# The order of the SBUF tiles in a dynamic convolution with two products behind it

## The chip, the cores and the metric

The kernel runs on one core of a Trainium2 chip. The metric is the device time of one execution in microseconds (us). It is given as the median of three runs.

## What is computed

The input `x` has 16384 tokens (4 sequences of 4096) of 192 channels. For each token and each of 8 heads a softmax over 7 weights is formed, and the token's 24 channels of the head become the weighted sum of the last 7 tokens (zeros ahead of a sequence). The result goes through two matrix products with a pointwise function between them, of 192 to 2048 to 192 channels:

```python
w = np.exp(w); w = w / (np.sum(w, axis=-1, keepdims=True) + 1e-09)
out = np.einsum('bshk,bskhg->bshg', w, x_unf)        # 7 taps
h = x @ w_in
g = np.where(h >= 1, h, np.where(h <= -1, 0.0, (h + 1) ** 2 / 4.0))
return (g @ w_out).astype(np.float32)
```

`w_in` and `w_out` come as 8-byte floats, all else as float32.

## The kernel before

**Tiling.** The tokens are cut into 32 blocks of 512, the 2048 hidden channels into 16 chunks of 128. A step of the main loop (index `w`) handles a pair of chunks of one block, so that there are 256 pairs, 8 for a block. Precision beyond one pass comes from splits into two parts: `hc` and `hl` are the high and low part of a block's transposed rows, `whi` and `wlo` those of `w_in`, `wo` holds both parts of `w_out` (192 + 192 columns for a chunk), `gh` and `gl` those of the hidden values.

**The first product** (`gemm1_pair`, L378) runs 9 passes for a pair: three thirds of the channels (64 rows each), and for each `whi` with `hc`, `wlo` with `hc`, `whi` with `hl`. A pass is two matmuls of 512 columns, one on either half of the array's rows. The weights are the operand that is loaded (128 columns, 512 bytes of a partition), `hc` or `hl` is the moving one (2048 bytes).

**The second product** (`gemm2_part`, L432) comes two pairs later. It runs 16 passes for a pair, again two matmuls each: `gh` is loaded and 384 columns of `wo` move (1536 bytes), then `gl` is loaded and 192 columns move. Two such passes are called a round here; there are 8 rounds for a pair.

**The other engines.** Between the two products ScalarE takes relu and square (L389, L392) and writes `gh` (L403), VectorE combines (L397) and writes `gl` (L404). GpSimd forms the convolution of a later block (L179, L189), VectorE transposes it in parts, SyncE issues all DMAs. In the first pairs the weights are decoded besides: 8 chunk buffers' worth of 8-byte floats are loaded into four buffers `r` (pool `raw`), and ScalarE and VectorE turn them into `whi`, `wlo` and `wo` by way of `head` and a PSUM bank `psw` (L327, L331, L340, L352, L356).

**What sets the order.** The order of each engine is written out by hand (`tc.manual_schedule()`), the tiles' buffers rotate within their pools.

**Where tiles lie.** The pools are laid out one behind another in the order in which they are opened, and within a pool the tiles in the order in which they are first asked for; each tile takes its bytes of a partition, rounded up to 32. The buffer `warm`, one float32, takes 32 bytes so, and what follows it starts at an odd multiple of 32.

Of the kernel before, what the change touches and what calls it, by code (L numbers as in the profile page):

```python
# [10 lines left out]
F32 = mybir.dt.float32  # L11
F32R = mybir.dt.float32r
U32 = mybir.dt.uint32
U16 = mybir.dt.uint16
BF16 = mybir.dt.bfloat16
F16 = mybir.dt.float16
AF = mybir.ActivationFunctionType
# [5 lines left out]
def kernel(  # L23
# [21 lines left out]
    nc = tc.nc  # L45
    P = 128
    B, S, D = x.shape
# [6 lines left out]
    Q = P // 2  # L54
# [18 lines left out]
    group_of = {b: (g, i) for g, bs in enumerate(groups) for i, b in enumerate(bs)}  # L73

    const = ctx.enter_context(tc.tile_pool(name="const", bufs=1))
    raw = ctx.enter_context(tc.tile_pool(name="raw", bufs=4))
    xp = ctx.enter_context(tc.tile_pool(name="xp", bufs=2))
    wp = ctx.enter_context(tc.tile_pool(name="wp", bufs=2))
    sp = ctx.enter_context(tc.tile_pool(name="sp", bufs=2))
# [2 lines left out]
    up = ctx.enter_context(tc.tile_pool(name="up", bufs=3))  # L82
    gp = ctx.enter_context(tc.tile_pool(name="gp", bufs=6))
    op = ctx.enter_context(tc.tile_pool(name="op", bufs=2))
    dram = ctx.enter_context(tc.tile_pool(name="dram", bufs=2, space=bass.MemoryType.DRAM))
    ps_h = ctx.enter_context(tc.tile_pool(name="ps_h", bufs=4, space=bass.MemoryType.PSUM))
    ps_o = ctx.enter_context(tc.tile_pool(name="ps_o", bufs=1, space=bass.MemoryType.PSUM))
# [2 lines left out]
    wr = wg.rearrange("b s h k -> (b s) (h k)")  # L90

    ident = const.tile([P, P], F32, tag="ident", name="ident")
    warm = const.tile([P, 1], F32, tag="warm", name="warm")
    ident16 = const.tile([P, P], BF16, tag="ident16", name="ident16")
    heads = [const.tile([P, (D // Q) * P + 2 * D, 2], U16, tag=f"head{m}", name="head") for m in range(2)]
    whi = const.tile([P, NF // 2, NC, P], F32R, tag="whi", name="whi")
    wlo = const.tile([P, NF // 2, NC, P], F32R, tag="wlo", name="wlo")
    wo = const.tile([P, NF, 2, D], F32R, tag="wo", name="wo")

    def run(ops):  # L100
        for o in ops:
            o()
# [28 lines left out]
    def load_w(g):  # L131
        bs = groups[g]
        t0, nb = bs[0] * N, len(bs)
        t = wp.tile([P, 2, n, H, K], F32, tag="w", name="w")
        nc.sync.dma_start(
            out=t[:, 0:nb].rearrange("p b j h k -> p b (j h k)"),
            in_=wr[t0:t0 + nb * N, :].rearrange("(b p j) e -> p b (j e)", p=P, j=n))
        w_t[g] = t
# [392 lines left out]
    with tc.manual_schedule():  # L531
        for t in heads:
            nc.vector.memset(t, 0)
        nc.gpsimd.memset(warm, 0.0)
        nc.scalar.activation(out=warm, in_=warm, func=AF.Exp)
        load_w(0)
        load_w(1)
        clear_x(0)
# [211 lines left out]
```

## Time and profile before

| | |
|---|---|
| runs | 1160.29, 1160.81, 1160.94 us |
| median | 1160.81 us |
| span of the profiled execution, first to last instruction | 1158.6 us |
| busy share of the span | PE 99%, weight loads 90%, ScalarE 83%, VectorE 72%, GpSimd 68% |
| granted TensorE clock | 1.00 in all but the first and last stretch |

The profile comes from one execution. Its own time from end to end is not given apart; its span is 2.2 us under the median of the runs. A matmul's busy time includes the stretch in which it drains beside the next one, so the distance from one start to the next, and not the duration, is a pass's share of the time.

### The profile page before, as it was taken

What the parts mean: (1) busy time and instruction counts of PE and PEld (TensorE: products, weight loads), DVE (VectorE), ACT (ScalarE), POOL (GpSimd) and SP (SyncE); (2) the same over time, 40 slices, a digit from 0 to 9 for tenths busy, and PEclk for the clock granted to TensorE, in tenths of its full rate; (3) what the DMA queues carried; (4) which work ended last, traced back from release to release, by engine and by line L of the source; (5) the groups of instructions that cost most, each with busy time, mean ns of one, the idle gap of its engine ahead of it and who ended that gap; (6) DMA issues with size and microseconds to landing.
All of it is one profiled execution on the core that took longest, in us unless ns stands there. A gap on an engine that the chain in (4) does not pass through costs nothing.

```text
span 1158.6 us, 32197 instructions
## 1 busy us (share of the span) xinstructions
PE 1145.0 (99%) x12885; PEld 1038.1 (90%) x12885; DVE 834.1 (72%) x1271; ACT 964.7 (83%) x1745; POOL 792.5 (68%) x511
## 2 busy tenths in 40 slices
PE   7999999999999999999999999999999999999998
PEld 5799999999999999999999999999999999999997
DVE  8887767677676776767777676776767767677664
ACT  6878888888888888888888888888888888888886
POOL 4788976667857678486686866678576785866310
PEclk9999999999999999999999999999999999999999
DMA  9422222212222212222121222222222122221100
GB/s 229 112 82 79 77 84 90 89 64 73 75 77 90 84 61 82 71 87 90 56 89 59 85 89 90 64 73 74 76 90 95 51 85 70 80 90 57 47 24 15
DMA packets 84052, 91.43 MB, mean 79 GB/s; under 512 B 5056, under 2 KB 75712, under 8 KB 83904
## 3 DMA queue, kind: packets, MB, share of 16 engines
q1 hardware_dynamic: 83904, 89.39, 24.0%
q8 instruction: 101, 1.65, 0.6%
q14 instruction: 47, 0.39, 0.1%
HBM read 64.99 MB, written 24.38 MB: 77 GB/s over the span
## 4 chain that ended last, share of the span: by engine, by line
PE 95%; ACT 2%; DMA 2%; DVE 1%; issue 0%; POOL 0%; DVEq 0%; POOLq 0%; ACTq 0%; SPq 0%
PE o L432 48%; PE psh L378 45%; DMA r<-in_moe_w_in_dram 1%; PE psx L267 1%; DMA r<-in_moe_w_out_dram 1%; PE psx L208 0%; ACT u L392 0%; DVE psh L397 0%; ACT u L389 0%; ACT gh L403 0%; DVE psw L340 0%; DVE gl L404 0%; POOL piece L189 0%; POOL acc L189 0%; ACT hc L258 0%
## 5 line engine op out<-in xcount | busy, mean ns | idle before, releaser
L432 PE MATMUL o<-wo,gh 64*128 64x384 f32 x4096 | 612.2, 355 | 1.5 <-SPq L441 1.4
L397 DVE SCALAR_TENSOR_TENSOR psh<-u,psh 128x512 f32<-128x512 f32 x512 | 354.7, 696 | 299.6 <-ACT u L392 299.4
L432 PE MATMUL o<-wo,gl 64*128 64x192 f32 x4096 | 542.7, 251 | 0.0
L432 PEld LDWEIGHTS o<-wo,gh 64*128 64x128 f32 x4096 | 421.1, 184 | 13.1 <-SPq L441 2.3
L432 PEld LDWEIGHTS o<-wo,gl 64*128 64x128 f32 x4096 | 421.3, 187 | 9.0
L389 ACT ACTIVATE u<-psh 128x512 f32<-128x512 f32 x512 | 301.5, 589 | 93.2 <-PE psh L378 91.2
L404 DVE TENSOR_TENSOR gl<-psh,gh 128x512 fp32r<-128x512 f32 x512 | 345.7, 686 | 15.3 <-ACT gh L403 1.1
L403 ACT ACTIVATE gh<-psh 128x512 fp32r<-128x512 f32 x512 | 299.2, 592 | 65.5 <-DVE psh L397 65.5
L378 PE MATMUL psh<-hc,whi 64*128 64x512 f32 x1536 | 349.8, 404 | 3.7 <-DVE wlo L356 1.9
L189 POOL TENSOR_TENSOR acc<-acc,pr 128x768 f32<-128x768 f32 x185 | 343.8, 1858 | 5.7 <-DVE head L331 2.0
L378 PE MATMUL psh<-hl,whi 64*128 64x512 f32 x1536 | 337.7, 391 | 0.0
L378 PE MATMUL psh<-hc,wlo 64*128 64x512 f32 x1536 | 337.3, 390 | 0.0
L392 ACT ACTIVATE u<-u 128x512 f32<-128x512 f32 x512 | 323.7, 632 | 16.0
L179 POOL TENSOR_TENSOR pr<-x,w 128x768 f32<-128x768 f32 x186 | 286.8, 1549 | 7.1 <-DVE psw L340 7.1
L259 POOL TENSOR_TENSOR hl<-XT,hc 128x512 fp32r<-128x512 f32 x90 | 115.4, 1297 | 221.2 <-ACT hc L258 221.2
L378 PEld LDWEIGHTS psh<-hl,whi 64*128 64x128 f32 x1536 | 173.6, 185 | 34.7 <-DVE hl L259 0.3
L378 PEld LDWEIGHTS psh<-hc,whi 64*128 64x128 f32 x1536 | 173.0, 185 | 29.4 <-DVE wlo L356 4.3
L378 PEld LDWEIGHTS psh<-hc,wlo 64*128 64x128 f32 x1536 | 174.1, 187 | 21.4
L179 POOL TENSOR_TENSOR acc<-x,w 128x768 f32<-128x768 f32 x31 | 47.9, 1547 | 72.5 <-DVE w L155 70.6
L258 ACT ACTIVATE hc<-XT 128x512 fp32r<-128x512 f32 x90 | 55.5, 618 | 0.0
L284 DVE STREAM_TRANSPOSE T<-acc 128x768 f32<-128x768 f32 x30 | 50.9, 1698 | 0.3 <-POOL acc L189 0.3
L457 DVE SCALAR_TENSOR_TENSOR osb<-o,osb 128x384 f32<-128x384 f32 x64 | 32.7, 556 | 2.7 <-ACT osb L456 2.7
(44 smaller groups left out, 188.8 us busy)
## 6 DMA issues: line engine op xcount, KB each, us to landing
x<-in_x_dram SPq DMA_DIRECT2D x28, 960.0 KB
XT<-D SPq DMA_DIRECT2D x180, 128.0 KB
out_dram<-osb SPq DMA_DIRECT2D x31, 384.0 KB
D<-T SPq DMA_DIRECT2D x30, 384.0 KB
x<-in_x_dram SPq DMA_DIRECT2D x4, 945.0 KB
w<-in_weight_gen_dram SPq DMA_DIRECT2D x15, 224.0 KB
r<-in_moe_w_in_dram SPq DMA_DIRECT2D x16, 192.0 KB
r<-in_moe_w_out_dram SPq DMA_DIRECT2D x8, 384.0 KB
```

Of the source, the lines that this page charges most:

```text
L179: held(eng.tensor_tensor(out=t, in0=xtile[:, k:k + n, :].rearrange("p j (h g) -> p j h g", h=H), in1=wt[:, gi, :, :, k:k + 1].to_broadcast ...
L189: held(eng.tensor_tensor(out=o, in0=s, in1=t, op=ALU.add))
L258: ops.append(lambda c=c: nc.scalar.activation(out=hc[:, c], in_=src[c], func=AF.Copy))
L259: ops.append(lambda c=c: lows.append(engines[c].tensor_tensor(out=hl[:, c], in0=src[c], in1=hc[:, c].bitcast(F32), op=ALU.subtract)))
L284: lambda: nc.vector.transpose(out=T.rearrange("p b c j -> p b j c"), in_=acc.rearrange("p j (r b) -> p b j r", b=R)),
L378: nc.tensor.matmul(out=pair[h][:, 0:N], lhsT=l[rows, f // 2, (c + h) % NC if b < 2 else c], rhs=r[rows, c], start=(s == 0), stop=(s == len ...
L389: nc.scalar.activation(out=u_t[i], in_=h_t[i][:, 0:N], func=AF.Relu, scale=0.5 * UNIT, bias=0.5)
L392: nc.scalar.activation(out=u_t[i], in_=u_t[i], func=AF.Square, scale=UNIT ** -0.5)
L397: nc.vector.scalar_tensor_tensor(out=pv, in0=uv, scalar=1.0 / UNIT, in1=pv, op0=ALU.min, op1=ALU.max)
L403: nc.scalar.activation(out=gh[:, 0:N], in_=gv, func=AF.Copy)
L404: nc.vector.tensor_tensor(out=gl[:, 0:N], in0=gv, in1=gh[:, 0:N].bitcast(F32), op=ALU.subtract)
L432: mm = nc.tensor.matmul(out=o_t[b][turn][:, k, 0:cols], lhsT=g_t[i][l][rows, t * P:(t + 1) * P], rhs=wo[rows, f].rearrange("p s d -> p (s ...
```

## The change

Three things are reordered, and one tile is widened. The pool of chunk buffers is opened last of the SBUF pools, so that it lies behind all others. In the pool of constants `ident16` comes ahead of `warm`, and the two `head` tiles behind the weights. `warm` grows from 1 to 32 floats, of which one is still used. No instruction is added or taken away, the order and the waits of each engine are the same, and so are all other sizes and numbers of buffers.

```diff
     const = ctx.enter_context(tc.tile_pool(name="const", bufs=1))
-    raw = ctx.enter_context(tc.tile_pool(name="raw", bufs=4))
     xp = ctx.enter_context(tc.tile_pool(name="xp", bufs=2))
...
     op = ctx.enter_context(tc.tile_pool(name="op", bufs=2))
+    raw = ctx.enter_context(tc.tile_pool(name="raw", bufs=4))
...
     ident = const.tile([P, P], F32, tag="ident", name="ident")
-    warm = const.tile([P, 1], F32, tag="warm", name="warm")
     ident16 = const.tile([P, P], BF16, tag="ident16", name="ident16")
-    heads = [const.tile([P, (D // Q) * P + 2 * D, 2], U16, tag=f"head{m}", name="head") for m in range(2)]
+    warm = const.tile([P, 32], F32, tag="warm", name="warm")
     whi = const.tile([P, NF // 2, NC, P], F32R, tag="whi", name="whi")
     wlo = const.tile([P, NF // 2, NC, P], F32R, tag="wlo", name="wlo")
     wo = const.tile([P, NF, 2, D], F32R, tag="wo", name="wo")
+    heads = [const.tile([P, (D // Q) * P + 2 * D + 0, 2], U16, tag=f"head{m}", name="head") for m in range(2)]
...
-        nc.gpsimd.memset(warm, 0.0)
-        nc.scalar.activation(out=warm, in_=warm, func=AF.Exp)
+        nc.gpsimd.memset(warm[:, 0:1], 0.0)
+        nc.scalar.activation(out=warm[:, 0:1], in_=warm[:, 0:1], func=AF.Exp)
```

Where the tiles start in the two built programs, in bytes of a partition (the first buffer, and the remainder that all buffers of the tile share):

| tile | before | remainder | after | remainder |
|---|---|---|---|---|
| `whi`, `wlo`, `wo` | 23456, 35744, 48032 | 416 mod 512 | 17408, 29696, 41984 | 0 mod 512 |
| `head` | 17312 | 416 mod 512 | 66560 | 0 mod 512 |
| `x`, `acc`, `pr`, `T` | 97312, 123936, 130080, 117792 | 32 mod 512 | 72704, 99328, 105472, 93184 | 0 mod 512 |
| `hc`, `hl` | 139296, 151584 | 32 mod 2048 | 114688, 126976 | 0 mod 2048 |
| `XT`, `u`, `piece` | 163872, 170016, 200736 | 32 mod 2048 | 139264, 145408, 176128 | 0 mod 2048 |
| `gh`, `gl` | 176160, 188448 | 32 mod 2048 | 151552, 163840 | 0 mod 2048 |
| the four `r` | 72608, 78784, 84960, 91136 | 32, 0, 32, 0 mod 64 | 202752, 208928, 215104, 221280 | 0, 32, 0, 32 mod 64 |

## Rows read from the trace of the kernel before

**Rows 1.** The page: span, and busy us (share of the span) xinstructions.

```profile
span 1158.6 us, 32197 instructions
PE 1145.0 (99%) x12885; PEld 1038.1 (90%) x12885; DVE 834.1 (72%) x1271; ACT 964.7 (83%) x1745; POOL 792.5 (68%) x511
```

**Rows 2.** The page: the chain that ended last, by engine and by line.

```profile
PE 95%; ACT 2%; DMA 2%; DVE 1%; issue 0%; POOL 0%; DVEq 0%; POOLq 0%; ACTq 0%; SPq 0%
PE o L432 48%; PE psh L378 45%; DMA r<-in_moe_w_in_dram 1%; PE psx L267 1%; DMA r<-in_moe_w_out_dram 1%; PE psx L208 0%; ACT u L392 0%; DVE psh L397 0%; ACT u L389 0%; ACT gh L403 0%; DVE psw L340 0%; DVE gl L404 0%; POOL piece L189 0%; POOL acc L189 0%; ACT hc L258 0%
```

**Rows 3.** Stretches: busy us of each engine, clock, DMA share and GB/s.

```profile
core 0: us, PE busy (x) PEld busy (x) DVE busy (x) ACT busy (x) POOL busy (x), PEclk, DMA share, GB/s
20.00:62.00 42.00, 37.60 (x361) 30.54 (x359) 37.36 (x68) 35.88 (x70) 29.95 (x19) 1.00 0.57 122
62.00:200.00 138.00, 137.65 (x1559) 126.31 (x1558) 100.50 (x150) 116.22 (x211) 112.45 (x71) 1.00 0.26 87
200.00:600.00 400.00, 400.00 (x4562) 366.47 (x4560) 287.77 (x434) 337.81 (x610) 293.12 (x188) 1.00 0.23 77
600.00:1000.00 400.00, 400.00 (x4560) 363.73 (x4558) 287.28 (x434) 337.49 (x608) 282.21 (x181) 1.00 0.23 78
```

**Rows 4.** Timeline of PE over one pair: start us, us, engine, line, operation.

```profile
600.22 0.42 PE L378 MATMUL psh<-hc,whi 64*128 64x512 f32 x2
600.48 0.39 PE L378 MATMUL psh<-hc,wlo 64*128 64x512 f32 x2
600.71 0.40 PE L378 MATMUL psh<-hl,whi 64*128 64x512 f32 x2
...
602.11 0.40 PE L378 MATMUL psh<-hl,whi 64*128 64x512 f32 x2
602.34 0.34 PE L432 MATMUL o<-wo,gh 64*128 64x384 f32 x2
602.51 0.25 PE L432 MATMUL o<-wo,gl 64*128 64x192 f32 x2
602.60 0.36 PE L432 MATMUL o<-wo,gh 64*128 64x384 f32 x2
602.80 0.25 PE L432 MATMUL o<-wo,gl 64*128 64x192 f32 x2
602.89 0.36 PE L432 MATMUL o<-wo,gh 64*128 64x384 f32 x2
...
604.61 0.42 PE L378 MATMUL psh<-hc,whi 64*128 64x512 f32 x2
```

**Rows 5.** The same for the weight loads, from the end of the first product.

```profile
602.11 0.19 PEld L432 LDWEIGHTS o<-wo,gh 64*128 64x128 f32 x2
602.34 0.19 PEld L432 LDWEIGHTS o<-wo,gl 64*128 64x128 f32 x2
602.52 0.19 PEld L432 LDWEIGHTS o<-wo,gh 64*128 64x128 f32 x2
602.62 0.19 PEld L432 LDWEIGHTS o<-wo,gl 64*128 64x128 f32 x2
602.80 0.19 PEld L432 LDWEIGHTS o<-wo,gh 64*128 64x128 f32 x2
602.91 0.19 PEld L432 LDWEIGHTS o<-wo,gl 64*128 64x128 f32 x2
```

**Rows 6.** By tile (`wo`, `r`): duration ns min/median/max, first and last start us.

```profile
L432 PEld LDWEIGHTS o<-wo,gh x4096: 182/184/189, 24.8 to 1152.9; 64*128 64x128 f32 x196
L432 PE MATMUL o<-wo,gh x4096: 332/358/444, 25.0 to 1153.1; 64*128 64x384 f32 x196
L432 PEld LDWEIGHTS o<-wo,gl x4096: 183/188/189, 25.0 to 1153.5; 64*128 64x128 f32 x196
...
L340 DVE SCALAR_TENSOR_TENSOR psw<-r,head x16: 555/558/580, 12.5 to 49.4; 128x384 uint32<-128x384 uint32 x16
L327 ACT ACTIVATE head<-r x7: 627/642/646, 11.8 to 48.2; 128x384 f16<-128x384 bf16 x7
```

## The prediction

> **What bounds the kernel now.** I read the busy shares first: TensorE (PE) is busy for 1145.0 of 1158.6 us, ScalarE for 83% and VectorE for 72% [rows 1]. The chain of waits agrees: 95% of the span is PE, 48% of it on the second product (L432) and 45% on the first (L378), so nearly nothing else ends a wait [rows 2]. [...] Only from 20 to 62 us is it busy for just 37.60 of 42.00 us, with DVE (37.36) and ACT (35.88) as full as PE [rows 3]. So what counts is the pace of PE in the steady part, and a little the work of DVE and ACT in the first 62 us.
>
> The steady pace is that of one pair of hidden chunks, 50 matmuls. The timeline has one pair start at 600.22 and the next at 604.61 [rows 4], 4.39 us. As a cross-check, 400 us hold 4562 matmuls, or 91.2 pairs, which is 4.38 us each [rows 3]; 256 pairs of 4.387 make 1123 of the 1158.6 us. Inside a pair: from 600.48 to 602.34 stand eight passes of the first product, two matmuls of 512 columns at once in each, so (602.34 - 600.48) / 8 = 0.2325 us a pass. The second product takes 604.61 - 602.34 = 2.27 us for eight rounds of a 384-column pass (gh) and a 192-column pass (gl), 0.284 a round. The first gh pass after the first product takes 602.51 - 602.34 = 0.17; the later ones 602.80 - 602.60 = 0.20, then gl 0.09 [rows 4]. The rows of the weight loads say why: the load for the next gh starts with the gl pass (602.52 and 602.80), the load behind it follows 0.10 to 0.11 us later (602.62, 602.91), so one load occupies the loader for about 0.11 us, longer than gl's 0.09. In the second product gl is thus hidden under a load, and every round costs a load plus a gh pass; in the first product a load (0.11) has half of a pass (0.23) to spare [rows 5].
>
> **The change part by part.** No instruction is added, removed or moved, and no wait: each engine's order is the same in both programs, every queue's too (SP's and POOL's DMAs and semaphores among them), and every tile has the same size and the same number of buffers. All that differs is where a tile starts. Before, every operand of the steady loop starts at 32 bytes past a multiple of 64, because the 4-byte tile `warm` took 32; the weights `whi`, `wlo`, `wo` lie at 416 past a multiple of 512, `hc`, `hl`, `gh`, `gl` at 32 past a multiple of 2048. After, these remainders are 0. The cost is therefore a price per read or write of each engine, times its count.
>
> PE, moving rows (`hc`, `hl` in the first product, `wo` in the second). The smallest unit for which the change can matter is 64 bytes, 16 float32 columns. [...] The trace gives no row of a moving float32 operand at another remainder mod 64, so this isn't excluded. What speaks against it: `wo` lies at four remainders mod 2048 as the chunk goes on (928, 416, 1952, 1440), a 384-column read crosses a multiple of 2048 from some and not from others, and the 4096 gh matmuls still have one duration (median 358 ns, of all their pairs) [rows 6]. The pairs' equal pace at 4.38 whatever ACT, DVE, POOL and DMA do at the time says that PE's reads meet no one else's. I take 0, as the nearest rows show no dependence on an address, with 17 x 6.7 x 256 = 29 us of gain as the bound on one side.
>
> PE, weights. The loads (0.10 to 0.11 us for 128 columns) [rows 5] are on the path in the second product alone. A gain there would need a load shorter than that; a loss would need a longer one (below). I take 0.
>
> [...]
>
> ACT, DVE and POOL. The chunk buffers are the one tile of the program that lies at both remainders before (32, 0, 32, 0 mod 64, read from 2 to 4 bytes further on). The 16 VectorE reads of them that write `psw` take 555 to 580 ns, median 558, the 7 ScalarE ones 627 to 646 [rows 6]: no two groups, a spread of under 4.5%. So the durations of these engines stay, in the decode stage from 20 to 62 us too, where they are on the path. If all their work on the path there changed by that spread, it would be under 2 us of 42; I take 0 with 1 us either way. In the steady part ACT has 400 - 337.8 = 62 us of slack in 400 [rows 3], which covers any such change. The DMAs write to other addresses; from 62 us on their engines are 23 to 26% busy [rows 3] and everything they load is used pairs later, so a change there is hidden.
>
> The sum: 0, against the profiled span of 1158.6 us, which lies 2.2 us under the median of 1160.81. Forecast **1160.8 us**.
>
> **The rivals.** [...] (b) **Slower: weights and moving rows now begin on the same remainder.** Before, a weight row starts 384 bytes (mod 512) away from a moving row; after, 0. If the two reads of PE then met and a load were stretched by one of its eight 64-byte units, that is 0.11 / 8 = 13.7 ns. In the first product the half-pass of slack swallows it; in the second every load behind gl is on the path from the first ns on: 8 x 13.7 x 256 = 28 us, 1188.9 us. For it: the load is the tightest link of the round [rows 5]. Against: loads and passes advance at different speeds (0.11 us for 128 columns, 0.23 for 512), so equal starts don't keep them equal, and passes of three lengths all meet loads now without a visible stretch: loads last 182 to 189 ns in all of the rows [rows 6]. [...] That the change doesn't do what it says is no rival: the built program has the tiles where the words put them.
>
> **How the numbers follow.** No change 0.57; (a) 0.28, since a fixed cost of the right size is there and unexplained; (b) 0.15. A measurement of this kernel tells about 0.2% (2.3 us) from no change. The no-change case with its 1 us at the start lies inside that. Range: from (a)'s one-unit time, 1131, to 1163, the upper edge of no change; it leaves out (b) and the two-unit form of (a), under 0.2. The forecast's own range is 1159 to 1163. Faster 0.28, within 0.2% 0.57, slower 0.15.
>
> **What would show it.** Right: the pair's step stays 4.39 us, a first-product pass 0.2325, a round 0.284, loads 0.10 to 0.11 apart. [...] (b): first-product passes unchanged, loads over 0.11 apart behind gl, rounds near 0.30. The prediction is wrong also if DVE's or POOL's durations move enough to show in the 5.2 us per pair of the first 62 us.

## The result and the profile after

The changed kernel takes 1146.94 us (median of 4 runs, 1145.49 to 1147.49), the kernel before 1160.70 us beside it. The ratio is 0.9874, with a 95% interval of 0.9861 to 0.9887: 13.8 us or 1.26% faster. The time lies inside the predicted range, but the likeliest case, no change, did not come about.

The page of the changed kernel, span and busy us, beside [rows 1]:

```profile
span 1145.6 us, 32197 instructions
PE 1130.8 (99%) x12885; PEld 1053.4 (92%) x12885; DVE 833.7 (73%) x1271; ACT 964.4 (84%) x1745; POOL 792.3 (69%) x511
```

The same instructions run, and DVE, ACT and POOL need the same time as before to within 0.4 us. PE's busy time falls by 14.2 us, the span by 13.0. By stretches (columns as in [rows 3]):

```profile
core 0: us, PE busy (x) PEld busy (x) DVE busy (x) ACT busy (x) POOL busy (x), PEclk, DMA share, GB/s
20.00:62.00 42.00, 37.77 (x343) 31.56 (x345) 36.40 (x68) 35.81 (x70) 28.81 (x19) 0.92 0.55 123
200.00:600.00 400.00, 400.00 (x4626) 388.16 (x4624) 291.62 (x441) 342.63 (x618) 296.98 (x189) 1.00 0.24 78
600.00:1000.00 400.00, 400.00 (x4618) 366.10 (x4616) 290.57 (x439) 342.87 (x618) 289.55 (x185) 1.00 0.24 79
```

PE is as full as before, and gets through 4618 to 4626 matmuls in 400 us where it was 4560 to 4562. Its timeline over one pair, to be laid beside [rows 4] (start us, us, operation):

```profile
599.55 0.41 PE L378 MATMUL psh<-hc,whi 64*128 64x512 f32 x2
599.81 0.40 PE L378 MATMUL psh<-hc,wlo 64*128 64x512 f32 x2
600.04 0.39 PE L378 MATMUL psh<-hl,whi 64*128 64x512 f32 x2
600.27 0.39 PE L378 MATMUL psh<-hc,whi 64*128 64x512 f32 x2
600.50 0.39 PE L378 MATMUL psh<-hc,wlo 64*128 64x512 f32 x2
...
601.40 0.39 PE L378 MATMUL psh<-hl,whi 64*128 64x512 f32 x2
601.63 0.33 PE L432 MATMUL o<-wo,gh 64*128 64x384 f32 x2
601.80 0.25 PE L432 MATMUL o<-wo,gl 64*128 64x192 f32 x2
601.89 0.36 PE L432 MATMUL o<-wo,gh 64*128 64x384 f32 x2
602.09 0.25 PE L432 MATMUL o<-wo,gl 64*128 64x192 f32 x2
602.17 0.36 PE L432 MATMUL o<-wo,gh 64*128 64x384 f32 x2
...
603.88 0.41 PE L378 MATMUL psh<-hc,whi 64*128 64x512 f32 x2
```

The first product takes 601.63 - 599.55 = 2.08 us (before 602.34 - 600.22 = 2.12), the second 603.88 - 601.63 = 2.25 (before 2.27), the pair 4.33 (before 4.39). From the fourth pass on (600.27) a pass of the first product takes (601.63 - 600.27) / 6 = 0.227 us, where the mean was 0.2325. The weight loads, beside [rows 5]:

```profile
601.80 0.19 PEld L432 LDWEIGHTS o<-wo,gh 64*128 64x128 f32 x2
601.91 0.19 PEld L432 LDWEIGHTS o<-wo,gl 64*128 64x128 f32 x2
602.09 0.19 PEld L432 LDWEIGHTS o<-wo,gh 64*128 64x128 f32 x2
602.20 0.19 PEld L432 LDWEIGHTS o<-wo,gl 64*128 64x128 f32 x2
```

They follow one another by 0.11 us after a gl pass has begun, as before. So the loads are no shorter; the passes are.

With the single starts of the trace, which are kept to 1 ns, the step from pair to pair can be had to 1 ns as a median over the steady pairs: 4.387 us before, 4.327 after. Of the 60 ns, 40 come from the first product (2.116 to 2.076) and 20 from the second (2.271 to 2.251). 248 pairs run at this pace, which is 248 x 0.060 = 14.9 us. The span gained 13.0, because in this execution the steady part began 1.8 us later (60.48 against 58.67 us); that is taken up at the end.

### The profile page after: what moved, and what is told of

It is laid out like the page before. It is cut to its first block, busy times and chain, and to the rows that moved or that the text cites. A ratio compares the mean times of both kernels' runs of the same rounds, so it can differ in the third digit from the quotient of the medians.

```text
span 1145.6 us, 32197 instructions
## 1 busy us (share of the span) xinstructions
PE 1130.8 (99%) x12885; PEld 1053.4 (92%) x12885; DVE 833.7 (73%) x1271; ACT 964.4 (84%) x1745; POOL 792.3 (69%) x511
## 4 chain that ended last, share of the span: by engine, by line
PE 90%; ACT 4%; DVE 2%; POOL 2%; issue 1%; DMA 1%; SPq 0%; DVEq 0%; POOLq 0%; ACTq 0%
PE o L432 46%; PE psh L378 44%; ACT u L392 1%; ACT u L389 1%; POOL acc L189 1%; DVE psh L397 1%; ACT gh L403 1%; PE psx L267 1%; DMA x<-in_x_dram 1%; POOL pr L179 1%; DVE gl L404 0%; ACT hc L258 0%; DVE s L153 0%; DVE psw L340 0%; ACT whi L352 0%
## 5 line engine op out<-in xcount | busy, mean ns | idle before, releaser
L432 PE MATMUL o<-wo,gl 64*128 64x192 f32 x4096 | 560.8, 247 | 0.0
L432 PEld LDWEIGHTS o<-wo,gh 64*128 64x128 f32 x4096 | 472.8, 184 | 9.0 <-SPq L441 1.0
L432 PEld LDWEIGHTS o<-wo,gl 64*128 64x128 f32 x4096 | 468.7, 188 | 5.5
L378 PE MATMUL psh<-hc,whi 64*128 64x512 f32 x1536 | 371.4, 397 | 4.2 <-DVE wlo L356 2.5
L378 PE MATMUL psh<-hc,wlo 64*128 64x512 f32 x1536 | 364.5, 390 | 0.0
L378 PE MATMUL psh<-hl,whi 64*128 64x512 f32 x1536 | 363.3, 389 | 0.0
L378 PEld LDWEIGHTS psh<-hc,whi 64*128 64x128 f32 x1536 | 200.3, 185 | 24.4 <-DVE wlo L356 4.1
L378 PEld LDWEIGHTS psh<-hl,whi 64*128 64x128 f32 x1536 | 200.1, 185 | 23.7 <-DVE hl L259 0.3
L378 PEld LDWEIGHTS psh<-hc,wlo 64*128 64x128 f32 x1536 | 200.3, 186 | 15.8
```

What stands on the lines that cost most here:

```text
L378: nc.tensor.matmul(out=pair[h][:, 0:N], lhsT=l[rows, f // 2, (c + h) % NC if b < 2 else c], rhs=r[rows, c], start=(s == 0), stop=(s == len ...
L432: mm = nc.tensor.matmul(out=o_t[b][turn][:, k, 0:cols], lhsT=g_t[i][l][rows, t * P:(t + 1) * P], rhs=wo[rows, f].rearrange("p s d -> p (s ...
```

## The experiments

Three theories were set against each other. A: a read that starts inside a 64-byte (or larger) unit costs PE time, so the remainder of each tile counts by itself, which is rival (a) of the prediction. B: the order of the pools counts. C: the distance between the operand that is loaded and the one that moves counts; C1 says that only the distance 0 is quick, C2 that the distance counts mod 64. In the following D1 is the start of `whi` less that of `hc`, D2 the start of `gh` less that of `wo`, both mod 512 (`wlo`, `hl` and `gl` have the same remainders as their partners). Before D1 is 384 and D2 is 128; in the changed kernel both are 0.

### All tiles by 32 bytes, and the old order at multiples of 64

`e1_all32` makes one tile of the changed kernel larger, so that all behind it moves by 32 bytes:

```diff
-    warm = const.tile([P, 32], F32, tag="warm", name="warm")
+    warm = const.tile([P, 40], F32, tag="warm", name="warm")
```

> The changed kernel, with `warm` 32 bytes larger, so that every tile behind it starts 32 bytes further on: weights at 32 mod 512, hc, hl, gh, gl at 32 mod 2048, in the changed order. Theory A (a read that starts inside a 64-byte unit costs PE time): the pair's step goes back to 4.387 us and the time to about 1160.8. Theory B (the order of the pools or the distance between tiles made the gain, not the remainder): the step stays at 4.327 and the time at about 1147. Theory C (what counts is where weights lie against moving rows: 384 bytes apart mod 512 before, 0 in the changed kernel and here): the step stays at 4.327.

`e2_before64` does in the kernel before what brings its tiles to multiples of 64, in the old order (the two lines that use `warm` take its first float, as in the change):

```diff
-    warm = const.tile([P, 1], F32, tag="warm", name="warm")
+    warm = const.tile([P, 16], F32, tag="warm", name="warm")
```

> The kernel before, in its own order, with `warm` of 16 floats (64 bytes) in place of 1: all tiles of the steady loop start at a multiple of 64 and of no more (weights at 448 mod 512, hc, hl, gh, gl at 64 mod 2048). Theory A with a unit of 64 bytes: step 4.327 us, time about 1147, as in the changed kernel. Theory A with a unit of 128 or more: step 4.387, time 1160.8. Theory B: 4.387. Theory C (distance 384 mod 512, as before): 4.387.

`e1_all32` took 1147.61 us, ratio 0.9882 (0.9866 to 0.9899): the whole gain, with every steady tile at 32 past a multiple of 64 again. `e2_before64` took 1161.08 us, ratio 0.9997 (0.9988 to 1.0007): nothing, with all of them at multiples of 64. The boundaries of the two products in `e1_all32` (start of a first product, of the second, of the next first):

```profile
802.16 0.41 PE L378 MATMUL psh<-hc,whi 64*128 64x512 f32 x2
804.23 0.33 PE L432 MATMUL o<-wo,gh 64*128 64x384 f32 x2
806.48 0.41 PE L378 MATMUL psh<-hc,whi 64*128 64x512 f32 x2
```

and in `e2_before64`:

```profile
802.41 0.42 PE L378 MATMUL psh<-hc,whi 64*128 64x512 f32 x2
804.53 0.34 PE L432 MATMUL o<-wo,gh 64*128 64x384 f32 x2
806.80 0.42 PE L378 MATMUL psh<-hc,whi 64*128 64x512 f32 x2
```

Steps of 4.32 and 4.39: pass for pass the first is the changed kernel and the second the kernel before. With that A falls: in `e1` every steady tile starts 32 bytes inside any unit of 64 or more, and the kernel is quick. B and C are left, since D1 and D2 are those of the changed kernel in the one and those of before in the other.

### One operand against the other

`e3_hchl32` moves the moving rows of the first product alone, `e4_whilo32` its weights alone (in `e3` a pad of 8 floats ahead of the pool of `hc` and one behind it, in `e4` the larger `warm` and a pad behind `wlo`; all else lies at multiples of 64):

```diff
-    cv = ctx.enter_context(tc.tile_pool(name="cv", bufs=2))
+    cv = ctx.enter_context(tc.tile_pool(name="cv", bufs=2)); ctx.enter_context(tc.tile_pool(name="pada", bufs=1)).tile([P, 8], F32, tag="pad", name="pad")
```

> The changed kernel with hc, hl and XT alone 32 bytes further on (all else at multiples of 64). If the moving rows of the first product carry their share of the gain, a first product takes 2.116 us (as before) in place of 2.076, the second stays at 2.251, and the step is 4.367. If the weights carry it, or the second product does, the step stays at 4.327. One look, so the step is what counts; the time would be near 1157 or 1147.

> The changed kernel with whi and wlo alone 32 bytes further on (all else at multiples of 64). If the start of a weight load matters, the first product goes from 2.076 to up to 2.116 us and the step to up to 4.367; since a load there has half a pass to spare, my theory is that it stays at 4.327 and the gain lies with the moving rows.

`e3_hchl32` took 1160.23 us and `e4_whilo32` 1155.19 (one run each). The boundaries in `e3_hchl32`:

```profile
802.25 0.41 PE L378 MATMUL psh<-hc,whi 64*128 64x512 f32 x2
804.37 0.34 PE L432 MATMUL o<-wo,gh 64*128 64x384 f32 x2
806.63 0.41 PE L378 MATMUL psh<-hc,whi 64*128 64x512 f32 x2
```

and in `e4_whilo32`:

```profile
803.07 0.41 PE L378 MATMUL psh<-hc,whi 64*128 64x512 f32 x2
805.18 0.33 PE L432 MATMUL o<-wo,gh 64*128 64x384 f32 x2
807.43 0.41 PE L378 MATMUL psh<-hc,whi 64*128 64x512 f32 x2
```

Moving either operand of the first product by 32 bytes against the other slows that product, from 2.076 to 2.12 and 2.11 us. My expectation for `e4`, that a load has half a pass to spare and its start can't matter, was wrong. For `e3` a step of 4.367 was expected, with the second product unchanged, and 4.387 came. The pads account for the second product: those of `e3` left `gh` and `gl` 64 bytes past `wo` (D2 = 64), those of `e4` left them level, and the second product took 2.262 us in `e3` and 2.252 in `e4`. B is out: both kernels have the order of the changed one.

### A scan of distances

Eight kernels, the two of the next part among them, set D1 and D2 in the changed kernel, by `warm`, by a pad behind `wlo` that brings `wo` and all behind it back to a multiple of 512, and by a pool ahead of `gh`. For `f1_w64_g32` (D1 = 64, D2 = 32):

```diff
-    warm = const.tile([P, 32], F32, tag="warm", name="warm")
+    warm = const.tile([P, 48], F32, tag="warm", name="warm")
...
-    wlo = const.tile([P, NF // 2, NC, P], F32R, tag="wlo", name="wlo")
+    wlo = const.tile([P, NF // 2, NC, P], F32R, tag="wlo", name="wlo"); const.tile([P, 112], F32, tag="pada", name="pad")
...
-    up = ctx.enter_context(tc.tile_pool(name="up", bufs=3))
+    up = ctx.enter_context(tc.tile_pool(name="up", bufs=3)); ctx.enter_context(tc.tile_pool(name="padg", bufs=1)).tile([P, 8], F32, tag="pad", name="pad")
```

The others have D1 / 4 more floats in `warm`, (512 - D1) / 4 in the pad behind `wlo` and D2 / 4 in the pool.

> The changed kernel with whi, wlo 64 bytes (mod 512) past hc, hl, and gh, gl 32 bytes past wo; moving rows stay at 0 mod 512. Theory C (PE's pace hangs on the distance between the loaded and the moving operand, mod 512 at most): both products change. C1 (only distance 0 is quick): first product 2.108 to 2.125 us (now 2.076), second 2.262 to 2.271 (now 2.251), step 4.37 to 4.39. C2 (what counts is the distance mod 64): first product 2.076, second about 2.27. Theory B (order of the pools): both as in the changed kernel, 4.327.

> The changed kernel with whi, wlo 128 bytes past hc, hl (mod 512), and gh, gl 256 past wo. C1: 2.108 to 2.125 and 2.262 to 2.271, step 4.37 to 4.39. C2 (mod 64), and likewise mod 128: 2.076 and 2.251, step 4.327. B: 4.327 too, so f1 tells C2 from B.

> The changed kernel with whi, wlo 256 bytes past hc, hl (mod 512), and gh, gl 480 past wo, that is 32 short of it. C1: 2.108 to 2.125 and 2.262 to 2.271. If the distance counts mod 256: 2.076 for the first, over 2.251 for the second. B: 4.327.

> The changed kernel with whi, wlo 64 bytes short of hc, hl (mod 512), and gh, gl 64 short of wo. C1: 2.108 to 2.125 and 2.262 to 2.271, step 4.37 to 4.39. If it counts which of the two is ahead, this run and f1 differ in the first product by 0.01 us or more. B: 4.327.

> whi, wlo 192 bytes (mod 512) past hc, hl and gh, gl 320 past wo. C1: slower than at distance 0 in both, first product over 2.08, second over 2.251, step 4.35 to 4.39. If some other distance is better than 0, it shows as a first product under 2.076 or a second under 2.251.

> whi, wlo 320 bytes (mod 512) past hc, hl and gh, gl 192 past wo. C1: first product over 2.08, second over 2.251, step 4.35 to 4.39. A better distance than 0 would show as under 2.076 or under 2.251.

All the kernels in one table. The products and steps are medians in us over the 247 steps from the first steady pair of each trace on, with both values where there are two paces; the time is a median of several runs for before, the changed kernel, e1, e2, g1 and g2, and one run for the others.

| kernel | D1 (mod 256) | D2 (mod 256) | first product | second | step | time |
|---|---|---|---|---|---|---|
| before | 384 (128) | 128 (128) | 2.116 | 2.271 | 4.387 | 1160.70 |
| e2 | 384 (128) | 128 (128) | 2.116 | 2.271 | 4.387 | 1161.08 |
| changed | 0 | 0 | 2.076 | 2.251 | 4.327 | 1146.94 |
| e1 | 0 | 0 | 2.076 | 2.251 | 4.327 | 1147.61 |
| e3 | 480 (224) | 64 | 2.125 | 2.262 | 4.387 | 1160.23 |
| e4 | 480 (224) | 0 | 2.108 | 2.252 | 4.360 | 1155.19 |
| f1 | 64 | 32 | 2.123 | 2.264 | 4.387 | 1160.12 |
| f2 | 128 | 256 (0) | 2.117 | 2.255 | 4.371 | 1157.32 |
| g1 | 384 (128) | 0 | 2.117 | 2.255 | 4.371 | 1157.20 |
| f3 | 256 (0) | 480 (224) | 2.098 | 2.275 | 4.373 | 1157.66 |
| f4 | 448 (192) | 448 (192) | 2.093 or 2.095 | 2.268 or 2.258 | 4.361 or 4.353 | 1154.77 |
| g3 | 192 | 320 (64) | 2.093 | 2.273 | 4.367 | 1157.04 |
| g4 | 320 (64) | 192 | 2.122 | 2.258 | 4.380 | 1158.72 |
| g2 | 0 | 128 | 2.118 or 2.082 | 2.268 or 2.278 | 4.387 or 4.360 | 1158.64 |

What follows from it: no distance that was tried is quicker than 0 in either product, so there was no better version than the changed kernel to run. C1 holds for the step with one correction, that the distance counts mod 256. `f2` and `g1` differ in both D1 (128 and 384) and D2 (256 and 0) and are the same mod 256; the means of their passes agree to 0.1 ns. Their boundaries, first `f2_w128_g256`:

```profile
800.08 0.42 PE L378 MATMUL psh<-hc,whi 64*128 64x512 f32 x2
802.20 0.34 PE L432 MATMUL o<-wo,gh 64*128 64x384 f32 x2
804.45 0.42 PE L378 MATMUL psh<-hc,whi 64*128 64x512 f32 x2
```

then `g1_w384`:

```profile
800.99 0.42 PE L378 MATMUL psh<-hc,whi 64*128 64x512 f32 x2
803.11 0.34 PE L432 MATMUL o<-wo,gh 64*128 64x384 f32 x2
805.36 0.42 PE L378 MATMUL psh<-hc,whi 64*128 64x512 f32 x2
```

`f1` with `g4` (D1 64 and 320) fit as well: their D2 differ, and still the passes of their first products agree to 0.2 ns (means over the pairs from 750 us on). So do those of `g3` and of every second pair of `f4` (D1 192 and 448). For D2 the pair of `f2` and `g1` is the only one. It isn't mod 128: by that `f2` and `g2` would be the changed kernel, 4.327, and their steps are 4.371 and 4.387 or 4.360. C2 falls with them, and with `f4` (4.361 or 4.353).

Two expectations of the scan failed. `f3` (D1 = 256) was to take 2.076 us for its first product if the distance counts mod 256, and took 2.098. Its last two passes take 226.7 ns, as in the changed kernel; passes before them are longer. `f4` took 2.093 or 2.095 where C1 had 2.108 to 2.125, which by the expectation of `f4` would mean that it counts which operand is ahead (`f1` took 2.123); their D2 differ too, but so do those within the pairs just named, so it is likely and not settled. The step of `f4` isn't one number either: from pair to pair it alternates between 4.361 and 4.353 us. So a product's time is not set by its own distance alone, and a row of the table is no price of one distance.

One rival to a distance has no run of its own: that each start counts by itself mod 256, with remainders of 0 and 32 both quick. No kernel has all four operands level at another remainder. Against it stand two rows: from the kernel before to `e2` the remainders mod 256 of `hc` and `gh` go from 32 to 64 and those of `whi` and `wo` from 160 to 192, and no product changes by 1 ns; and in `e4` `gh` and `wo` lie level at 64, and the second product takes 2.252 us.

### Each product by itself

`g1_w384` gives the first product its old distance and leaves the second at 0, `g2_g128` the other way round (made as above, with 384 and 0, and 0 and 128).

> Undoes the change for the first product alone: whi, wlo lie 384 bytes (mod 512) past hc, hl, as in the kernel before; gh, gl and wo stay at distance 0. Theory C1: first product 2.116 us as before, second 2.251 as in the changed kernel, step 4.367; 248 steady pairs x 0.040 = 9.9 us over the changed kernel's 1147, near 1157. If the two products can't be told apart so (what one loses shifts the other), the step differs from 4.367 by 0.01 or more.

> Undoes it for the second product alone: gh, gl lie 128 bytes (mod 512) past wo, as in the kernel before; whi, wlo and hc, hl stay at distance 0. C1: first product 2.076, second 2.271, step 4.347; 248 x 0.020 = 5.0 us over 1147, near 1152. The two runs' losses then add up to the change's gain of 0.060 us per pair.

`g1_w384` took 1157.20 us (1156.14 to 1157.79, ratio 0.9959, 0.9946 to 0.9972), as expected. `g2_g128` took 1158.64 us (1155.87 to 1163.61, ratio 0.9977, 0.9960 to 0.9993) in place of 1152. The pace in its profiled execution isn't one pace. Boundaries of `g2_g128` in the first half and further on:

```profile
402.17 0.47 PE L378 MATMUL psh<-hc,whi 64*128 64x512 f32 x2
404.29 0.37 PE L432 MATMUL o<-wo,gh 64*128 64x384 f32 x2
406.55 0.47 PE L378 MATMUL psh<-hc,whi 64*128 64x512 f32 x2
...
699.62 0.41 PE L378 MATMUL psh<-hc,whi 64*128 64x512 f32 x2
701.70 0.34 PE L432 MATMUL o<-wo,gh 64*128 64x384 f32 x2
703.98 0.41 PE L378 MATMUL psh<-hc,whi 64*128 64x512 f32 x2
```

At 400 us a pair takes 406.55 - 402.17 = 4.38 us, at 700 703.98 - 699.62 = 4.36. Each holds for many pairs to within a ns, 4.360 for 127 of them and 4.387 for 109. By the single starts the pace changes four times before 323 us, goes from 4.387 to 4.360 at 529 us, with one pair of 4.557 between, and back at 983. Pairs of 4.4 to 5.3 us also come in the other kernels, and all but `f4` keep their pace through them to within 3 ns. The longer rows at 400 us (0.47 against 0.41) show that the two matmuls of a pass, one on either half of the array, start 44 ns apart there. That doesn't make the pace: from 988 us on they start 4 ns apart and the step is 4.387 again. In the slower of the two the first product takes 2.118 us although its own operands lie level. So the products can't be priced apart: undoing the first costs 44 ns a pair, undoing the second 33 to 60, and both together 60. The expectation for `g1` had named this as its second case; in `g1` the step came within 0.004 of the first case (4.371 for 4.367), and in `g2` it missed by 0.013 or 0.040.

## Why the prediction held its range and missed its middle

**What bounds the kernel** was right. The whole gain is PE's pace in the steady part, and the other engines' slack covered all else (from 200 to 600 us DVE is busy for 291.62 and ACT for 342.63 of 400 us).

**The step that failed is "PE, moving rows: I take 0".** In its place the runs showed 0.060 us a pair, 40 ns in the first product and 20 in the second. The 29 us beside it, and with them the lower edge of the range, rest on a term, 6.7 ns for each of 17 passes of a pair, that no run shows. What they show is that the mean of eight passes of the first product went from 0.2325 to (601.63 - 599.81) / 8 = 0.2275 us, while the later gh passes still take 602.09 - 601.89 = 0.20. The step rested on two readings. The first was that `wo` lies at four remainders mod 2048 and its matmuls still have one duration [rows 6]. That row gives 332 to 444 ns about one median and doesn't part the four, but more than that was amiss. All four (928, 416, 1952, 1440) are 416 mod 512, and `gh` and `gl` lie at 32 mod 2048 throughout. The distance between the two was thus 128 in every one of the 4096 matmuls, and the rows could not show that it counts. The second was that an even pace means that PE's reads meet no one else's. For GpSimd and the DMAs that holds up: in the kernel before, in the stretch below (columns as in [rows 3]), GpSimd works for 3.88 of 45 us and the DMA share is 0.05, and the step up to 1140 us is 4.387 us as elsewhere.

```profile
1100.00:1145.00 45.00, 45.00 (x520) 41.01 (x518) 28.30 (x43) 37.42 (x68) 3.88 (x3) 1.00 0.05 16
```

For ACT and DVE it isn't shown: they work for 37.42 and 28.30 of the same 45 us. And an even pace says nothing on the one read that always comes at the same time: PE's own weight load, which starts with the pass (the loads at 602.52 and 602.80 in [rows 5] with the gl passes at 602.51 and 602.80 in [rows 4]) and so can cost the same each time.

**Rival (a)**, that a moving read which starts inside a unit of 64 bytes costs one unit more, had the sign, not the mechanism. `e1` and `e2` show that the remainder that it spoke of has no effect here: in the changed order the step is 4.327 us with every steady tile at 32 past a multiple of 64 as with all at 0, in the old order 4.387 at either. Its 29 us are twice the 13.8 that came. That the time lies in the predicted range is therefore luck: the range reaches down to 1131 us only for the sake of (a).

**Rival (b)** named what counts, the distance between weights and moving rows, and had the sign wrong: level is the quickest of all that were tried, where it feared a stretch. (It gave 384 bytes as the distance before; in the second product, where it put the price, it was 128.) It looked for the price in the loads of the second product, with the first one safe behind half a pass of slack. The loads kept their 0.11 us, and two thirds of the gain came from the first product, 40 of 60 ns. So it is the passes that got shorter, in the product where the loads had slack; that the distance holds up the pass that is running, and not the load, is argued from this.

That a distance has a price is measured: in `g1` only the start of `whi` and `wlo` against all else differs mod 512 from the changed kernel, and the step goes from 4.327 to 4.371 us. Why it has one isn't shown: a load starts when a pass does (in the kernel before, 600.48 and 600.71 us for both in the first product), and no run reads with one of them alone.

**ACT, DVE and POOL at no cost** was right. The reads of the chunk buffers, beside [rows 6], with the buffers at 0, 32, 0, 32 mod 64 in place of 32, 0, 32, 0:

```profile
L340 DVE SCALAR_TENSOR_TENSOR psw<-r,head x16: 555/560/572, 13.7 to 51.2; 128x384 uint32<-128x384 uint32 x16
L327 ACT ACTIVATE head<-r x7: 625/637/648, 13.0 to 50.0; 128x384 f16<-128x384 bf16 x7
```

Medians of 560 and 637 ns against 558 and 642.

**The first 62 us, put at 1 us either way,** came out 1.8 us later in the profiled execution: the steady part begins at 60.48 us where it was 58.67. The views give two pieces. The first transposes wait for the convolution's first products, which wait for `x` (the first line is a row of PE's timeline, the next two are of the waits from 0 to 62 us, the last is the stretch from 30 to 37.3 us):

```profile
9.08 6.77 PE L267 MATMUL psx<-ident,piece 128*128 128x128 f32 x60 [1.50 <-DVE piece L227]
```

```profile
POOL piece L227 <- DMA x<-in_x_dram: 2.4, 1, 2.4
DVE piece L227 <- DMA x<-in_x_dram: 1.0, 1, 1.0
```

```profile
30.00:37.30 7.30, 6.50 (x36) 5.58 (x38) 6.18 (x13) 6.08 (x13) 4.92 (x3) 0.53 1.08 226
```

They begin at 9.08 us (8.14 before), and later the granted clock is lower, 0.53 as the mean from 30 to 37.3 us (1.00 before). Ahead of the fall PE was as busy as in the kernel before (from 18 to 30 us for 8.44 us, 8.39 before), and from 33 to 37.3 us, at a clock of 0.50, it was busy throughout (4.30 of 4.30 us). Neither piece goes with the change for sure: `e1`, in the same order of tiles, begins its steady part at 59.01 us at a clock of 1.00 in all of that time, `g1`, slower in its pace, begins the transposes as late as the changed kernel (9.11 us), and the clock fell for 3.4 us in `f4` and `g2` as well (means of 0.997 and 0.998 over the execution). What delays `x` in some executions wasn't tried.

**The chances.** Faster had 0.28, on the strength of a fixed cost in each pass. No run shows such a cost: the traces give a pass of the first product as a whole, 0.2325 us before and 0.2275 after, and not what part of it is fixed.

## What to carry to other kernels

Where TensorE is the bound and its pace is the same from step to step, ask what else moves in step with it before reading the evenness as freedom from conflict: here its own weight loads did. Compare the starts of the loaded and the moving tile mod 256, and try them level; here that took no instruction, brought the step from 4.387 to 4.327 us and was worth 1.26%. To learn whether an address counts by itself, move everything by the same amount; if nothing happens, move one operand against the other.

## What the runs showed of the hardware that was not expected

In this kernel the pace of the float32 matmuls hangs on the distance mod 256 between the loaded and the moving operand (`f2` and `g1`, which differ by 256 in both, are at 4.371 each): with 64 rows on either half of the array the step of 50 matmuls was 4.327 us with both products at distance 0 and 4.353 to 4.387 at the others tried, and a shift of 32 bytes is enough to see it (`e4`, 4.360). It does not hang on the remainder of both together, 0 or 32 (4.327 both). Nor does it hang on how far apart the two halves of the array run: in the changed kernel the two matmuls of a pass start some 150 ns apart from 327 to 556 us and 3 ns apart from 738 us on, and the step is 4.327 in both stretches.

The cost doesn't sit in the one product whose operands are apart. In `g2_g128`, whose first product is level, that product took 2.118 us in some stretches of one execution and 2.082 in others. How one product hands its delay to the next is left open.
